# A fused attention, Fourier and gating kernel: batch 1's Fourier stage by radix 6 and 3, and GpSimd's products on VectorE

## The chip, the cores and the metric
One Trainium2 chip, one core of it. The metric is device microseconds of one launch. Engines in the text: PE (TensorE), DVE (VectorE), ACT (ScalarE), POOL (GpSimd), SP (which starts DMAs). Each engine runs its own list of instructions in order, so an instruction that waits holds back all behind it on that engine.

## What is computed
The reference runs three layers on 2 batches of 768 tokens. The first is a linear attention with decay over 8 heads of 48 features:

```
for t in range(S):
    cur = einsum('bhd,bhe->bhde', u * kt, vt)
    y[:, :, t] = einsum('bhd,bhde->bhe', rt, state + cur)
    state = wt[..., None] * state + einsum('bhd,bhe->bhde', kt, vt)
```

The second mixes by a Fourier transform over tokens and features, of which only the real part is kept, then normalises and runs an MLP (384 to 1536 to 384):

```
u  = x + real(fft(fft(x, axis=1), axis=2))
un = (u - mean(u)) / sqrt(var(u) + 1e-6)
x  = u + maximum(un @ w_ch1, 0) @ w_ch2
```

The third is a gated MLP: `h = gelu(x @ w_in)`, split in two halves, the second of them normalised and multiplied over the tokens by a 768x768 matrix `w_sg`, then `x + (u * v_s) @ w_out`. Inputs are 64-bit floats for the weights of the second and third layer.

## The kernel before, in words
**Precision.** Most of the large products are done as three passes over operands that are split in a high part (rounded, by ACT) and a low part (the difference): hi x hi, hi x lo, lo x hi. `divide` makes the two parts of the weights: a 64-bit weight arrives by DMA in `raw` (384 columns) or `w_raw` (768 columns), three DVE operations on its words (L170 to L172) make a 32-bit number in `st`, ACT copies it into `w.hi`, and POOL subtracts for `w.lo` (L177). There is one `st` tile, so the next weight's L170 can only begin when L177 has read it.

**Attention.** The heads go in pairs, four for each batch (n = 0 to 3 are batch 0, n = 4 to 7 batch 1). `prep` of a pair loads decays P (112x774), r and k (`rk`, or in one tile with P: XE, XO, prk) and v, and makes on DVE a scan of the decays (L232), a product with r (L245), and two products that make k (L249, L250); k times the inverse decays (L247) is on DVE for n = 0, 1 and on POOL for the others. `own_term` makes what a token takes from itself: for n >= 4 two products over `prod` on POOL (L264, L266), a sum on DVE (L267), and `times_v` on POOL (L279); for n < 4 by matmuls, a copy by ACT and `times_v` on POOL. `scores` are matmuls, an ACT copy and a mask by POOL (L294). `chunk_states` are transposes and matmuls, with a short scan on DVE (L319); `values` are matmuls and one addition on DVE (L344), half a pair at a time. `butterfly` adds and subtracts the halves of the tokens (L349, L350), with a high part by ACT and a low part by POOL (L352).

**Fourier stage.** `fourier` takes a batch through matrices of cosines and sines: 54 matmuls of 386 or 384 columns over the tokens (`x_ps`), 36 of 256 columns that put the own tokens in place (`t_ps`), and 72 of 192 or 194 columns over the features (`d_ps`).

**MLP of the second layer (`moe1`).** It goes over halves of a batch (384 tokens). A block is 9 matmuls of 384 columns into `z_ps`, a rounding by ACT (`z_hi`, L530), a difference by DVE (`z_lo`, L531), and 9 matmuls into `ch`. The third layer (`gating`) comes last.

**Order.** Written down, it is: batch 0's attention (span's start to about 75 us in the trace); batch 0's Fourier stage with the first steps of moe1 (75 to 101), whose instructions keep their written order, `first_through` being the last of them; then `merge(first(), second(), FR)`, which takes moe1's blocks of batch 0 in turn with the steps of batch 1: its attention (101 to 214) and its Fourier stage (214 to 262.6); then moe1 of batch 1, during which the weights `win` and `wsg` of the third layer are loaded and split, and the gating. Within this a scheduler with modelled times sets each engine's list, and it counts a tile's reuse and `behind(x, first_through)` as bounds. All of batch 1's preparation is held behind `first_through`; `attention` prepares one pair ahead (two at n = 0) and never beyond the running batch.

**Names the change touches:** KV and PV (which pairs have L247 and L264 on DVE), `divide` L177, `own_term` L266, `times_v` L279, `values` L344, `butterfly`, `attention`, `fourier` for batch 1, and the tables `tdft` (batch 0 and 1) in `load_tdft`.

Of the kernel before, what the change touches and what calls it, by code (L numbers as in the profile page):

```python
# [93 lines left out]
def fused(ctx, tc, ins, out, dbg=None):  # L94
# [104 lines left out]
    def prep(n, b, p, ap):  # L199
# [24 lines left out]
        for c0, c1 in parts:  # L224
# [98 lines left out]
    def values(b, c0, rt, sc, v, dv, U):  # L323
# [758 lines left out]
```

## Time and profile before

| what | value |
|---|---|
| median of 3 runs | 485.19 us (483.95 to 487.18) |
| the profiled execution's own time | 485.52 us |
| its span, first to last instruction | 483.7 us (1.8 us lie around it) |
| mean granted TensorE clock | 0.947 |
| busy: PE, DVE, POOL, ACT | 433.6, 274.0, 182.1, 172.7 us |
| chain that ended last: PE, DVE, issue, POOL, DMA, ACT | 55, 15, 10, 6, 5, 4% |

The profile is of one execution. Busy shares are means over stages with different limits, so the stretches are read apart: batch 0's attention, its Fourier stage, batch 1's attention with moe1 of batch 0, batch 1's Fourier stage, and what follows. A busy time of DVE or POOL includes time in which the other of the two held it up; a busy PE includes matmuls that wait in its pipe.

### The profile page before, as it was taken

The numbers are of one execution on the slowest core, as the hardware profiler recorded it, in microseconds if no ns is written. First come the engines' busy times: TensorE is split into PE (matmuls) and PEld (weight loads), VectorE is DVE, ScalarE is ACT, GpSimd is POOL, SyncE is SP. The second block draws the span as 40 slices with busy tenths as digits, with TensorE's granted clock in tenths as the row PEclk, the third lists the DMA queues.
The fourth block names the chain that finished last, engine by engine and source line by source line (L and its number), as shares of the span: only waits on it lengthen the run. The fifth ranks groups of instructions, "written<-read, shape, count | busy, mean of one in ns | idle before, by whom it ended". The sixth has DMA issues, their size and how long they took to land.

```text
span 483.7 us, 6884 instructions
## 1 busy us (share of the span) xinstructions
PE 433.6 (90%) x2662; PEld 408.3 (84%) x2662; DVE 274.0 (57%) x453; ACT 172.7 (36%) x369; POOL 182.1 (38%) x182
## 2 busy tenths in 40 slices
PE   8778788876789688999999799999998999999994
PEld 8667787765678678899999699999987998999994
DVE  4857387389986978634044963541158734711332
ACT  2435355452344236444322532431355413311110
POOL 2857553154786967320000341200446524200330
PEclk9659899897979989999999899999999999999998
DMA  8948534036035223013000041000243100110002
GB/s 213 251 146 265 166 119 130 0 101 242 0 119 176 91 67 110 1 40 91 1 0 2 1 131 33 1 0 1 66 114 88 61 1 1 43 56 1 0 20 87
DMA packets 14074, 36.75 MB, mean 76 GB/s; under 512 B 1808, under 2 KB 5680, under 8 KB 13648
## 3 DMA queue, kind: packets, MB, share of 16 engines
q1 hardware_dynamic: 13456, 32.54, 22.5%
q0 software_dynamic: 576, 3.68, 2.2%
q8 instruction: 23, 0.38, 0.3%
q14 instruction: 19, 0.16, 0.1%
HBM read 33.86 MB, written 2.36 MB: 75 GB/s over the span
## 4 chain that ended last, share of the span: by engine, by line
PE 55%; DVE 15%; issue 10%; POOL 6%; DMA 5%; ACT 4%; SPq 1%; POOLq 0%; ACTq 0%; DVEq 0%
PE s_ps L107 10%; PE ch L107 8%; PE z_ps L107 8%; PE o_ps L107 5%; PE u_ps L107 4%; PE d_ps L107 3%; PE x_ps L107 3%; PE v_ps L107 3%; PE t_ps L426 2%; PE y_ps L342 2%; DMA raw<-in_wsg 2%; DVE st L171 2%; DVE st L170 2%; DVE st L172 1%; DMA w_raw<-in_w 1%
## 5 line engine op out<-in xcount | busy, mean ns | idle before, releaser
L107 PE MATMUL ch<-z_hi,w 128*128 128x384 f32 x288 | 84.5, 355 | 3.9 <-DVE uT L541 2.3
L107 PE MATMUL z_ps<-us_hi,w 128*128 128x384 f32 x288 | 82.5, 348 | 0.8 <-ACT us_hi L506 0.5
L107 PEld LDWEIGHTS ch<-z_hi,w 128*128 128x128 f32 x288 | 55.4, 199 | 6.0 <-ACT z_hi L530 2.7
L107 PE MATMUL ch<-z_lo,w 128*128 128x384 f32 x144 | 51.3, 356 | 10.2 <-DVE z_lo L531 10.2
L531 DVE SCALAR_TENSOR_TENSOR z_lo<-z_ps,z_hi 128x384 fp32r<-128x384 f32 x48 | 26.4, 552 | 55.7 <-ACT z_hi L530 55.7
L107 PEld LDWEIGHTS z_ps<-us_hi,w 128*128 128x128 f32 x288 | 54.1, 193 | 2.2 <-ACT us_hi L506 0.8
L107 PE MATMUL z_ps<-us_lo,w 128*128 128x384 f32 x144 | 49.4, 343 | 0.0
L530 ACT ACTIVATE z_hi<-z_ps 128x384 fp32r<-128x384 f32 x48 | 23.4, 490 | 57.0 <-PE z_ps L107 43.8
L107 PEld LDWEIGHTS ch<-z_lo,w 128*128 128x128 f32 x144 | 28.5, 198 | 12.4 <-DVE z_lo L531 12.1
L623 POOL TENSOR_TENSOR vn_lo<-t_g,vn_hi 128x384 fp32r<-128x384 f32 x16 | 16.1, 1014 | 57.1 <-ACT vn_hi L622 57.1
L619 DVE SCALAR_TENSOR_TENSOR t_g<-s_ps,g,bsg 128x384 f32<-128x384 f32 x16 | 9.5, 615 | 43.6 <-PE s_ps L107 43.6
L294 POOL TENSOR_SCALAR_AFFINE_SELECT sc<-sc 128x384 f32<-128x384 f32 x32 | 29.5, 939 | 12.0 <-ACT sc L293 12.0
L342 PE MATMUL y_ps<-v,sc 128*128 128x120 f32 (+1 forms) x192 | 34.0, 301 | 0.0
L177 POOL TENSOR_TENSOR w<-st,w 128x384 fp32r<-128x384 f32 (+1 forms) x18 | 24.4, 1363 | 24.0 <-ACT w L176 23.9
L107 PE MATMUL s_ps<-wsg_hi,vn_lo 128*128 128x384 f32 x96 | 32.3, 336 | 0.0
L107 PE MATMUL s_ps<-wsg_hi,vn_hi 128*128 128x384 f32 x96 | 32.3, 336 | 0.0
L107 PE MATMUL s_ps<-wsg_lo,vn_hi 128*128 128x384 f32 x96 | 32.3, 336 | 0.0
L483 POOL TENSOR_TENSOR z_lo<-uc,z_hi 128x384 fp32r<-128x384 f32 x7 | 7.8, 1120 | 60.0 <-ACT z_hi L482 59.9
L342 PEld LDWEIGHTS y_ps<-v,sc 128*128 128x128 f32 x192 | 28.6, 209 | 1.2 <-issue 0.8
L107 PEld LDWEIGHTS z_ps<-us_lo,w 128*128 128x128 f32 x144 | 27.9, 194 | 0.0
L177 POOL TENSOR_TENSOR wsg_lo<-raw,wsg_hi 128x384 fp32r<-128x384 f32 x12 | 12.4, 1038 | 33.2 <-ACT wsg_hi L176 33.2
L622 ACT CAST vn_hi<-t_g 128x384 fp32r<-128x384 f32 x16 | 8.0, 513 | 38.9 <-DVE t_g L620 28.0
(261 smaller groups left out, 1060.0 us busy)
## 6 DMA issues: line engine op xcount, KB each, us to landing
raw<-in_w SPq DMA_DIRECT2D x12, 384.0 KB, 3.4
w_raw<-in_w SPq DMA_DIRECT2D x12, 384.0 KB, 4.5
raw<-in_win SPq DMA_DIRECT2D x8, 384.0 KB, 3.8
prod<-in_ruk SPq DMA_DIRECT2D x4, 624.0 KB, 4.6
tdft<-in_tdft POOLq DMA_DIRECT2D x2, 1158.0 KB, 6.8
v<-in_v SPq DMA_DIRECT2D x8, 288.0 KB, 5.7
raw<-in_wsg SPq DMA_DIRECT2D x12, 192.0 KB, 2.4
out<-o SPq DMA_DIRECT2D x12, 192.0 KB, 1.9
```

The costliest lines, as they stand in the source:

```text
L107: nc.tensor.matmul(o, lhsT=x, rhs=y, start=start and i == 0, stop=stop and i == len(ps) - 1, **kw)
L170: behind(nc.vector.tensor_scalar(out=st, in0=top, scalar1=3, scalar2=0x3FFFFFF8, op0=ALU.logical_shift_left, op1=ALU.bitwise_and), first_t ...
L171: nc.vector.scalar_tensor_tensor(out=st, in0=top, scalar=0xC0000000, in1=st, op0=ALU.bitwise_and, op1=ALU.bitwise_or)
L177: nc.gpsimd.tensor_tensor(out=w.lo[to], in0=x, in1=w.hi[to].bitcast(F32), op=ALU.subtract)
L294: nc.gpsimd.affine_select(out=sc, in_=sc, pattern=[[0, 3], [1, C]], compare_op=ALU.is_gt, fill=0.0, base=0, channel_multiplier=-1)
L342: nc.tensor.matmul(y3[:, i, to], lhsT=sc[h][:, i, :], rhs=vf[:, of], start=c == 0, stop=True, skip_group_check=c > 0)
L426: nc.tensor.matmul(o, lhsT=l, rhs=r, start=i == 0, stop=i == len(parts) - 1)
L530: nc.scalar.activation(out=z.hi, in_=z_ps, func=AF.Relu)
L531: nc.vector.scalar_tensor_tensor(out=z.lo, in0=z_ps, scalar=0.0, in1=z.hi.bitcast(F32), op0=ALU.max, op1=ALU.subtract)
L619: nc.vector.scalar_tensor_tensor(out=t, in0=s_ps[h], scalar=g[:, f:f + 1], in1=bsg[:, hs], op0=ALU.mult, op1=ALU.add)
L622: nc.scalar.copy(vn.hi[:, f, 3 * h:3 * h + 3], th)
L623: nc.gpsimd.tensor_tensor(out=vn.lo[:, f, 3 * h:3 * h + 3], in0=th, in1=vn.hi[:, f, 3 * h:3 * h + 3].bitcast(F32), op=ALU.subtract)
```

## The change
Five things change.

1. POOL's products move to DVE: L247 for all pairs (KV), L264 for all of batch 1 (PV), L266, `times_v` (which for n < 4 now reads the matmuls' result without ACT's copy), and the low parts of weights in `divide`.
2. The first two pairs of batch 1 (AP = 2) are prepared while batch 0's third and fourth pair run. Only later pairs' scans stay behind `first_through`; `dec` goes into the tile "kn", and there is a fourth `ends`.
3. Batch 1's `values` write straight into a tile of the whole batch, and `radix6` takes the place of `butterfly`: seven DVE additions a pair, none on ACT or POOL.
4. `fourier_by_radix` takes the place of `fourier` for batch 1: 18 transposes for the own tokens, `radix3` for three groups of frequencies (four DVE operations each), a split (high by ACT, low by DVE, 768 columns), 54 matmuls of 256 columns over the tokens, and 36 of 256 columns over the features, with the sums into `uT` on DVE.
5. Its table `dft6` (2.36 MB) is loaded once batch 0's Fourier stage has left the tile of `tdft`, by a DMA that POOL starts.

```diff
-KV = range(2)
+KV = range(8)
+AP = 2
-PV = range(1)
+PV = (0, *range(4, 8))
...
     def divide(w, to, x):
         nc.scalar.copy(w.hi[to], x)
-        nc.gpsimd.tensor_tensor(out=w.lo[to], in0=x, in1=w.hi[to].bitcast(F32), op=ALU.subtract)
+        nc.vector.tensor_tensor(out=w.lo[to], in0=x, in1=w.hi[to].bitcast(F32), op=ALU.subtract)
...
-            if b:
+            if n >= NP + AP:
                 behind(scan, first_through)
...
-            behind(own, first_through, mybir.DependencyClass.Sync)
-            nc.gpsimd.tensor_tensor(out=r, in0=r, in1=u.to_broadcast([C, NC_, 2 * D]), op=ALU.mult)
+            if n >= NP + AP - 1:
+                behind(own, first_through)
+            nc.vector.tensor_tensor(out=r, in0=r, in1=u.to_broadcast([C, NC_, 2 * D]), op=ALU.mult)
...
-        nc.scalar.copy(dg[:, :, :, 0], dg_ps[:, :2 * NC_].rearrange("p (c h) -> p c h", h=2))
-        times_v(dv, dg, v)
+        times_v(dv, dg_ps[:, :2 * NC_].rearrange("p (c h o) -> p c h o", h=2, o=1), v)
...
     def times_v(dv, dg, v):
-        nc.gpsimd.tensor_tensor(...)
+        nc.vector.tensor_tensor(...)
...
+        to = made(b)[0][:, c0:c0 + 3, es].rearrange("p i (h e) -> p i h e", h=2) if b else own
+        return nc.vector.tensor_tensor(out=to, in0=yh, in1=own, op=ALU.add)
...
+    def radix6(x, y, Z, es):
+        ya, yb = y[:, 0:3, es], y[:, 3:6, es]
+        nc.vector.tensor_tensor(out=x[:, 1, 0:3:2], in0=ya[:, 0:3:2], in1=yb[:, 0:3:2], op=ALU.subtract)
+        nc.vector.tensor_tensor(out=x[:, 1, 1], in0=yb[:, 1], in1=ya[:, 1], op=ALU.subtract)
+        nc.vector.tensor_tensor(out=x[:, 0, 0:3], in0=ya, in1=yb, op=ALU.add)
+        nc.vector.tensor_tensor(out=x[:, :, 3], in0=x[:, :, 1], in1=x[:, :, 2], op=ALU.add)
+        nc.vector.scalar_tensor_tensor(out=Z[:, 2:4, es], in0=x[:, :, 3], scalar=-0.5, in1=x[:, :, 0], op0=ALU.mult, op1=ALU.add)
+        nc.vector.tensor_tensor(out=Z[:, 4:6, es], in0=x[:, :, 1], in1=x[:, :, 2], op=ALU.subtract)
+        nc.vector.tensor_tensor(out=Z[:, 0:2, es], in0=x[:, :, 0], in1=x[:, :, 3], op=ALU.add)
...
-            for m in range(len(ready) + n, min(n + (3 if n == 0 else 2), (b + 1) * NP)):
+            for m in range(len(ready) + n, min(n + (3 if n in (0, NP - 2, NP - 1) else 2), len(pairs))):
...
+    def fourier_by_radix(b, ap, y, Z, uT, sdft, ddft):
+        yr = ap([C, NC_, C], "yr")
+        nc.scalar.copy(yr, y[:, :, DM - 1::-3])
+        for f in range(3):
+            for h in range(2):
+                t_ps = gps.tile([C, 512], F32, name="t_ps", tag="g")
+                for i in range(3):
+                    c = 3 * h + i
+                    nc.tensor.transpose(t_ps[:, i * C:(i + 1) * C], yr[:, c, :] if f == 2 else y[:, c, f::3], ident)
+                ...
+        yield
+        ...
+        def radix3(g):
+            W = Z[:, groups[g][0]].rearrange("p z (c j) -> p z c j", c=3)
+            s = ap([C, 2, C], "t")
+            nc.vector.tensor_tensor(out=s, in0=W[:, :, 1], in1=W[:, :, 2], op=ALU.add)
+            nc.vector.tensor_tensor(out=W[:, :, 2], in0=W[:, :, 1], in1=W[:, :, 2], op=ALU.subtract)
+            nc.vector.scalar_tensor_tensor(out=W[:, :, 1], in0=s, scalar=-0.5, in1=W[:, :, 0], op0=ALU.mult, op1=ALU.add)
+            nc.vector.tensor_tensor(out=W[:, :, 0], in0=W[:, :, 0], in1=s, op=ALU.add)
+            return W
+        def parts(n, W):
+            Ws = Split(ap([C, 2, 3, C], "Wh", F32R), ap([C, 2, 3, C], "W", F32R))
+            nc.scalar.copy(Ws.hi, W)
+            nc.vector.tensor_tensor(out=Ws.lo, in0=W, in1=Ws.hi.bitcast(F32), op=ALU.subtract)
+            return Ws
+        ...
+        for n, g in enumerate(order):          # order = (1, 2, 0)
+            ...
+            for w in range(3):
+                x_ps = gps.tile([C, 2, 2, C], F32, name="x_ps", tag="g")
+                ...                            # 6 mm3, of 256 columns, per w over the groups
+                nc.scalar.copy(X[w].hi[:, xo], x_ps[:, xi])
+                nc.vector.tensor_tensor(out=X[w].lo[:, xo], in0=x_ps[:, xi], in1=X[w].hi[:, xo].bitcast(F32), op=ALU.subtract)
+            prepare()
+            yield
+            ...
+            for f in range(2):                 # 2 mm3 for f = 0, 4 for f = 1, twice
+                ...
+                nc.scalar.copy(hs, gh[:, 1])
+                nc.vector.tensor_tensor(out=ds[:, 0], in0=gh[:, 0], in1=hs, op=ALU.subtract)
+                ...
+                nc.vector.tensor_tensor(out=to, in0=to, in1=ds[:, 0:k], op=ALU.add)
+                ...
+            yield
...
+        t = sh.tile([C, 2, 6, 3, C], F32R, name="dft6", tag="tdft")
+        nc.gpsimd.dma_start(out=t, in_=ins["dft6"].bitcast(F32R))
...
-            yield from fourier(1, f1_room, back, made(1), X1, uT[1], range(3))
+            yield from fourier_by_radix(1, f1_room, *made(1), uT[1], dft6[:, :, 0:2], dft6[:, :, 2])
```

The change also moves instructions within the lists, at three places that the prediction speaks of. The same code lies 2 or 3 lines further down in the changed kernel up to `chunk_states` (L170 is L172, L177 is L179, L245 is L247, L247 is L249, L266 is L269), 4 in `values` and `butterfly`, and 122 in moe1.

**DVE in the second half of batch 0's attention.** Before, from the first pair's butterfly on (XO holds r and k of n = 3, `raw` weights of moe1):

```order
L350 TENSOR_TENSOR kn<-dv 128x288
L344 TENSOR_TENSOR dv<-y_ps,dv 128x288
L249 SCALAR_TENSOR_TENSOR y_379,unit<-XO,y_379 112x768
L250 SCALAR_TENSOR_TENSOR XO<-y_379,XO 112x768
L319 SCALAR_TENSOR_TENSOR kn<-kn,dec 112x288
L344 TENSOR_TENSOR dv<-y_ps,dv 128x288
L349 TENSOR_TENSOR kn<-dv 128x288
L350 TENSOR_TENSOR kn<-dv 128x288
L344 TENSOR_TENSOR dv<-y_ps,dv 128x288
L170 TENSOR_SCALAR st<-raw 128x384
L171 SCALAR_TENSOR_TENSOR st<-raw,st 128x384
L170 TENSOR_SCALAR st<-raw 128x384
```

With the change, from the second pair's butterfly on (`prk` holds P, r and k of n = 5, `dg_ps` belongs to n = 3):

```order
L353 TENSOR_TENSOR kn<-dv 128x288
L354 TENSOR_TENSOR kn<-dv 128x288
L234 SCALAR_TENSOR_TENSOR prk<-prk,d_91 112x774
L281 TENSOR_TENSOR dv<-v,dg_ps 128x576
L247 SCALAR_TENSOR_TENSOR prk<-prk 112x768
L172 TENSOR_SCALAR st<-raw 128x384
L249 TENSOR_TENSOR prk<-prk,y_567 112x768
L173 SCALAR_TENSOR_TENSOR st<-raw,st 128x384
L172 TENSOR_SCALAR st<-raw 128x384
L251 SCALAR_TENSOR_TENSOR y_567,unit<-prk,y_567 112x768
L174 SCALAR_TENSOR_TENSOR st<-raw,st 128x384
L173 SCALAR_TENSOR_TENSOR st<-raw,st 128x384
```

The scan of the decays of n = 5 (L234) and the products that follow from it (L247, L249, L251) have come here, between batch 0's own work and its weights; before, all of batch 1's preparation stood behind `first_through`.

**DVE where moe1's blocks begin to run beside batch 1's attention.** Before (`w_raw` and `st` hold weights, `prod` r, k and u of a pair of batch 1, `var`, `rstd` and `uc` belong to moe1's normalisation):

```order
L245 SCALAR_TENSOR_TENSOR rk<-rk,P 112x768
L531 SCALAR_TENSOR_TENSOR z_lo<-z_ps,z_hi 128x384
L497 TENSOR_TENSOR uc<-uc,uT_84 128x384
L267 TENSOR_REDUCE dg<-prod 128x12
L170 TENSOR_SCALAR st<-w_raw 128x768
L249 SCALAR_TENSOR_TENSOR y_958,unit<-P,y_958 112x768
L171 SCALAR_TENSOR_TENSOR st<-w_raw,st 128x768
L250 SCALAR_TENSOR_TENSOR rk<-y_958,rk 112x768
L232 SCALAR_TENSOR_TENSOR prk<-prk,d_91 112x774
L172 SCALAR_TENSOR_TENSOR st<-w_raw,st 128x768
L520 SCALAR_TENSOR_TENSOR var<-var,rstd 128x384
L245 SCALAR_TENSOR_TENSOR prk<-prk 112x768
```

With the change:

```order
L269 TENSOR_TENSOR prod<-prod 128x576
L619 TENSOR_TENSOR uc<-uc,uT_84 128x384
L653 SCALAR_TENSOR_TENSOR z_lo<-z_ps,z_hi 128x384 x2
L270 TENSOR_REDUCE dg<-prod 128x12
L172 TENSOR_SCALAR st<-w_raw 128x768
L281 TENSOR_TENSOR dv<-v,dg 128x576
L173 SCALAR_TENSOR_TENSOR st<-w_raw,st 128x768
L174 SCALAR_TENSOR_TENSOR st<-w_raw,st 128x768
L179 TENSOR_TENSOR w_977<-st,w_977 128x768
L642 SCALAR_TENSOR_TENSOR var<-var,rstd 128x384
L172 TENSOR_SCALAR st<-w_raw 128x768
L643 SCALAR_TENSOR_TENSOR var<-var,rstd 128x384
```

The preparation (L245, L249, L250, L232) is gone from here; the products over `prod` and v (L269, L281) and the low parts of the weights (L179) have come from POOL.

**DVE at the start of batch 1's Fourier stage.** With the change (`AL` holds the six radix outputs Z, `prod` the low parts of a group):

```order
L517 TENSOR_TENSOR AL<-AL 128x2x128
L173 SCALAR_TENSOR_TENSOR st<-raw,st 128x384
L518 SCALAR_TENSOR_TENSOR AL<-sc,AL 128x2x128 x2
L173 SCALAR_TENSOR_TENSOR st<-raw,st 128x384
L653 SCALAR_TENSOR_TENSOR z_lo<-z_ps,z_hi 128x384
L644 SCALAR_TENSOR_TENSOR rstd<-var,rstd 128x384
L518 SCALAR_TENSOR_TENSOR AL<-sc,AL 128x2x128
L174 SCALAR_TENSOR_TENSOR st<-raw,st 128x384
L519 TENSOR_TENSOR AL<-AL,sc 128x2x128 x2
L174 SCALAR_TENSOR_TENSOR st<-raw,st 128x384
L519 TENSOR_TENSOR AL<-AL,sc 128x2x128
L525 TENSOR_TENSOR prod<-AL,P 128x768
```

Before, at this place stood the two butterfly additions of the last pair and then at once the low part of the first `x_ps`. Now `radix3` of three groups (L516 to L519) and five operations on weights (L172 to L174) stand ahead of the first low parts L525.

## Rows read from the trace of the kernel before

**Rows 1.** Busy time of each engine by stretch of the span.
```profile
core 0: us, PE busy (x) PEld busy (x) DVE busy (x) ACT busy (x) POOL busy (x), PEclk, DMA share, GB/s
0.00:75.00 75.00, 61.22 (x463) 54.79 (x463) 49.37 (x64) 30.64 (x68) 42.55 (x53) 0.84 0.68 196
...
101.00:214.00 113.00, 90.83 (x603) 80.87 (x601) 91.36 (x119) 46.07 (x96) 72.25 (x52) 0.92 0.29 97
214.00:262.60 48.60, 48.60 (x310) 48.60 (x310) 15.91 (x38) 14.74 (x36) 2.45 (x2) 1.00 0.12 33
262.60:320.00 57.40, 53.92 (x292) 52.04 (x291) 36.87 (x75) 23.06 (x50) 16.42 (x15) 0.97 0.12 35
```

**Rows 2.** Groups of DVE, 101 to 214 us; last column: idle before, releaser.
```profile
L170 DVE TENSOR_SCALAR st<-w_raw 128x768 uint32<-128x768 uint32 x6 | 6.5, 1078 | 2.3 <-POOL w L177 2.3
...
L344 DVE TENSOR_TENSOR dv<-y_ps,dv 128x288 f32<-128x288 f32 x7 | 3.1, 444 | 5.5 <-PE y_ps L342 5.5
...
L170 DVE TENSOR_SCALAR st<-raw 128x384 uint32<-128x384 uint32 x4 | 1.3, 352 | 3.3 <-POOL w L177 2.8 <-DMA raw<-in_w 0.5
```

**Rows 3.** Groups of POOL, 101 to 214 us, that the change leaves there.
```profile
L294 POOL TENSOR_SCALAR_AFFINE_SELECT sc<-sc 128x384 f32<-128x384 f32 x16 | 14.5, 918 | 4.0 <-ACT sc L293 4.0
...
L483 POOL TENSOR_TENSOR z_lo<-uc,z_hi 128x384 fp32r<-128x384 f32 x3 | 3.2, 1050 | 2.5 <-ACT z_hi L482 2.4
L511 POOL TENSOR_TENSOR uc<-uc 128x384 f32<-128x384 f32 x2 | 2.0, 1010 | 0.1
L510 POOL TENSOR_TENSOR uc<-uc 128x384 f32<-128x384 f32 x2 | 2.0, 1006 | 14.8 <-ACT uc L509 14.8
```

**Rows 4.** Timeline of DVE: start, us, operation, idle before.
```profile
117.53 1.75 DVE L232 TENSOR_TENSOR_SCAN prk<-prk,d 112x774 f32<-112x774 f32 x1
119.21 0.93 DVE L172 SCALAR_TENSOR_TENSOR st<-w_raw,st 128x768 uint32<-128x768 uint32 x1
120.06 0.55 DVE L520 SCALAR_TENSOR_TENSOR var<-var,rstd 128x384 f32<-128x384 f32 x1
120.53 0.94 DVE L245 SCALAR_TENSOR_TENSOR prk<-prk 112x768 f32<-112x768 f32 x1
...
123.20 3.73 DVE L170 TENSOR_SCALAR st<-w_raw 128x768 uint32<-128x768 uint32 x1 [0.66 <-POOL w L177]
```

**Rows 5.** Timeline of POOL beside the last row of the group before.
```profile
123.12 1.54 POOL L247 TENSOR_TENSOR prk<-prk,y 112x768 f32<-112x768 f32 x1
...
125.11 1.40 POOL L264 TENSOR_TENSOR prod<-prod 128x576 f32<-128x576 f32 x1
```

**Rows 6.** Chain that ended last: start, us, engine and line.
```profile
44.84 1.15 POOL dv L279
45.99 1.50 POOL XO L247
...
55.78 5.96 DMA raw<-in_w
...
223.35 1.60 PE x_ps L107 x9
224.96 2.04 PE t_ps L426 x12
226.99 1.56 PE z_ps L107 x9
...
236.75 1.99 PE d_ps L107 x18
```

**Rows 7.** Timeline of DVE, end of batch 1's attention.
```profile
214.23 0.46 DVE L344 TENSOR_TENSOR dv<-y_ps,dv 128x288 f32<-128x288 f32 x1 [1.27 <-PE y_ps L342]
...
218.85 0.36 DVE L170 TENSOR_SCALAR st<-raw 128x384 uint32<-128x384 uint32 x1 [2.29 <-DMA raw<-in_win]
```

**Rows 8.** DMA issues: KB each, median us from issue to landing.
```profile
rk<-in_rk SPq DMA_DIRECT2D x2, 672.0 KB, 4.8
...
XO<-in_rk SPq DMA_DIRECT2D x1, 672.0 KB, 14.3
```

More of the change, by code (lines that the diff above doesn't have):

```diff
@@ L250, in prep @@
             ready_k.append(nc.vector.scalar_tensor_tensor(out=k, in0=flat(y0), scalar=2.0, in1=k, op0=ALU.subtract, op1=ALU.mult))
-        ends = all_ends[n % 3]
+        ends = all_ends[n % 4]
         nc.scalar.copy(ends[:, 0:NC_ - 1], P[:, 0:NC_ - 1, C])
@@ L313, in chunk_states @@
                 nc.tensor.matmul(kv_ps[r0:r1, c * D:c * D + C], lhsT=kn[:, c, r0:r1], rhs=vf[:, o:o + C], start=True, stop=True)
-        us = ap([PR, D, NC_], "kn")
+        both = ap([PR, 2, D, NC_], "kn")
+        us, dec = both[:, 0], both[:, 1]
+        nc.scalar.copy(dec, ends[:, None, :].to_broadcast([PR, D, NC_]))
         nc.scalar.copy(us, kv_ps[:, :NC_ * D].rearrange("p (c e) -> p e c", c=NC_))
-        nc.scalar.copy(dec[:, :, 0:NC_ - 1], ends[:, None, 0:NC_ - 1].to_broadcast([PR, D, NC_ - 1]))
         chain = us.rearrange("p e c -> p (e c)")
@@ L369, in tail @@
                 region = len(nc.cur_bb.bb.instructions)
-            gate = values(b, 3, rt, sc[2:], v, dv, states[n % 2])
-            butterfly(ap, dv, made(b), slice(p * 2 * D, (p + 1) * 2 * D), nc.vector if b == 0 and p == NP - 1 else nc.gpsimd)
+            gate = values(b, 3, rt, sc[2:], v, dv, states[n % 2], slice(p * 2 * D, (p + 1) * 2 * D))
+            es = slice(p * 2 * D, (p + 1) * 2 * D)
+            if b:
+                radix6(ap([C, 2, 4, 2 * D], "kn"), *made(b), es)
+            else:
+                butterfly(ap, dv, made(b), es, nc.vector if p == NP - 1 else nc.gpsimd)
             through(b, p)
@@ L392, in attention @@
             yield
-            values(b, 0, rt, sc[:2], v, dv, states[n % 2])
+            values(b, 0, rt, sc[:2], v, dv, states[n % 2], slice(p * 2 * D, (p + 1) * 2 * D))
             last = (n, b, p, rt, sc, v, dv)
@@ L850, in fused @@
         states = [sh.tile([PR, NC_ - 1, 2 * D], F32, name=f"U{i}") for i in range(2)]
-        all_ends = [sh.tile([PR, NC_], F32, name=f"ends{i}") for i in range(3)]
-        dec = sh.tile([PR, D, NC_], F32, name="dec")
-        for t in (*states, *all_ends, dec):
+        all_ends = [sh.tile([PR, NC_], F32, name=f"ends{i}") for i in range(4)]
+        for t in (*states, *all_ends):
             nc.gpsimd.memset(t, 0.0)
@@ L862, in fused @@
         a_room = room(att.enter_context(tc.tile_pool(name="att", bufs=1)), CFG1)
-        f1_room = room_of(a_room, ps="v", su="dv")
+        f1_room = room_of(a_room, yr="y0", Wh="P", W="prod", Xh="rk", t="sc", ds="dv")
         parts, X0 = {}, [[], []]
@@ L867, in made @@
             if b not in parts:
-                parts[b] = parts_of(f_room if b == 0 else a_room)
+                parts[b] = parts_of(f_room) if b == 0 else [a_room([C, NC_, DM], t) for t in ("AH", "AL")]
             return parts[b]
@@ L1003, in _constants @@
         fd[:, 2 * i], fd[:, 2 * i + 1] = np.cos(ph), -np.sin(ph)
+    k3 = -math.sqrt(3.0) / 2
+    cols = []
+    for r, z in ((0, "r"), (3, "r"), (1, "r"), (1, "i"), (2, "r"), (2, "i")):
+        th = 2 * np.pi * ((p[:, None] * (6 * p[None, :] + r)) % S) / S
+        c, s = np.cos(th), np.sin(th)
+        g = k3 if r == 2 else -k3
+        cols.append(np.concatenate([c, s], 1) if z == "r" else g * np.concatenate([s, -c], 1))
+    sd = np.stack(cols, 1)
+    ph0 = 2 * np.pi * ((p[:, None] * (3 * p[None, :])) % DM) / DM
+    ph1 = 2 * np.pi * ((p[:, None] * (3 * p[None, :] + 1)) % DM) / DM
+    dd = np.stack([np.cos(ph0), np.sin(ph0), np.cos(ph1), k3 * np.sin(ph1), -k3 * np.cos(ph1), np.sin(ph1)], 1)
     half = np.zeros((C, 2, 2, 2, C // 2), np.float32)
```

68 lines of the change are left out of this document (58 added, 10 removed).

## The prediction, made before the changed kernel had run

> **What bounds the kernel now.** I read first the busy table by stretch [rows 1], to see which engine is full where. Four stretches matter. In batch 0's attention (0 to 75 us) no engine is full: PE 61.2, DVE 49.4 and POOL 42.6 of 75. In batch 1's attention beside moe1 (101 to 214, 113 us) DVE is busy 91.4, PE 90.8, POOL 72.3. In batch 1's Fourier stage (214 to 262.6) PE is busy all of 48.6. After that PE has 53.9 of 57.4, DVE 36.9.
>
> Second, the groups of DVE in the second stretch [rows 2]: part of its 21.6 us of idle time ends on POOL (2.3 and 2.8, both times the first step of the next weight, which waits until POOL has read `st`), 5.5 on PE's result of the values. Third, DVE's timeline [rows 4]. Where nothing disturbs it, a 774-wide scan takes 1.68 us from its start to the next start, a 768-wide operation 0.85, a 384-wide one 0.47; I use 0.07 + columns/960 us for other widths. But the one-input L170 of 768 columns, at 123.20, took 3.73, over four times the price of the two-input operation of that width, and beside it POOL ran L247 and L264 [rows 5]. So DVE's busy time contains waiting that POOL causes. Priced at the quiet rates, the 116 operations that DVE runs in that stretch would take 65.4 us, not 91.4: 26 us are stretch. Fourth, the chain [rows 6] for what orders batch 0's attention and the Fourier stage.
>
> **The change, part by part.**
>
> *A, batch 0's attention and Fourier stage (0 to 101).* By the new order DVE runs 84 operations up to the end of the attention instead of 58; the added ones (preparation of n = 4 and 5, k of n = 2 and 3, four `times_v`, low parts of weights) cost 20 us at quiet prices, against 25.6 of idle. The chain loses POOL's `times_v` and k, 1.15 and 1.50 [rows 6], for 0.67 and 0.85 on DVE: about 1.2 here, and as much again where the same pair of steps recurs. But near 55 us the chain passes to a DMA of weights (5.96), and n = 5's preparation now stands in front of those weights' DVE work, which gives most of it back. I take −1. Bounds: −2.7 (POOL's steps vanish, nothing comes back), and +16, if of the 20 us only the 4 of removed stretch are covered; I am near the low end because idle time exceeds the addition and DVE is the only engine that gets work.
>
> *B, batch 1's attention beside moe1 (113 us).* DVE's list from the first block to the last addition of the values, at quiet prices:
> - was 65.4
> - preparation of n = 4 and 5, now in A: −8.9; butterflies −2.6; small operations of the normalisation and sums that fall on the other side of the cut −2.6
> - three radix6 of seven operations +5.6; k for n = 6 and 7 +1.7; products over `prod` +4.0; `times_v` +2.0; ten low parts of weights +7.1
>
> The sum is 71.7, say 72. To it comes what stretch is left. POOL keeps its masks and the LayerNorm pieces, 14.5 + 3.2 + 2.0 + 2.0 = 21.7 us [rows 3] of 72.3; taking stretch in proportion, 26 x 21.7/72.3 = 7.8. Of the idle 21.6, the 5.1 behind POOL go [rows 2]; 16.5 stay, since PE's results come no sooner. That makes 72 + 7.8 + 16.5 = 96, or −17. Bounds: no idle at all gives 80, −33; PE's own work speaks against that (90.8 busy, though that contains waiting). On the other side, all of POOL's 21.7 stops DVE: 72 + 21.7 + 16.5 = 110, −3. I take −17, the proportional case: what POOL keeps are short operations (0.9 to 1.05 us [rows 3]) spread over the stretch, where the removed ones ran in pairs, 1.54 and 1.40 one behind the other [rows 5].
>
> *C, batch 1's Fourier stage (48.6 us).* PE spends 6 x 1.60 on `x_ps`, 3 x 2.04 on `t_ps` and 4 x 1.99 on `d_ps`: 23.7 us [rows 6]; moe1's blocks take the rest and stay. The change makes 90 matmuls of 256 columns. From 1.60/9 = 0.178 for 386 columns, a 256-wide one is 0.12 (bounds: 0.111, the 192-wide ones of `d_ps`, and 0.170, the 256-wide ones of `t_ps`): 10.8, and 18 transposes in 6 groups at 0.16: 2.9. PE saves 10. But the operands now come by DVE: from the last value to the first low part (L525) stand 24 or so operations, namely radix6 (1.9), radix3 of three groups (4.0), a weight pair (2.4), rows of the normalisation (1.4) and two of 0.55 and 0.86, about 12 us, and that weight pair has to wait for its DMA: in the kernel before DVE idled 2.3 us for it at 218.85, all 4.6 us from the last values to it in hand [rows 7]. PE has 2.9 us of transposes and 3.2 of one block (18 matmuls at 1.56/9 [rows 6]) to cover it. I count 5.5 of waiting and 2 more where a group's gh, hs and sums run one after the other with one block to hide them. −10 + 7.5 = −2.5, say −3. Bounds −9.5 (0.5 exposed) and +4.3 (the whole 12 and a DMA of 2.3 exposed).
>
> *D, after 262.6.* 24 low parts of 384 columns go to DVE at 0.47, 11 us of work, on an engine busy for 36.9 of 57.4 [rows 1]; PE, with 53.9 of 57.4, sets the end. 0; if that idle cover of 20 us were gone, part of the 11 would show: bounds −2 and +4. The table's DMA of 2.36 MB starts after batch 0's Fourier stage, in a stretch whose DMA share is 0.29 [rows 1], more than 100 us ahead of its use: 0.
>
> Sum: −1 − 17 − 3 + 0 = −21, so a span of 462.7; with the 1.8 around it 464.5. The profiled execution is 0.3 us above the median of 485.19, so the median of the new kernel comes to **464**.
>
> **A rule of the chip against it.** The row at 123.20 shows DVE slowed by POOL, with an operation that has a single input. The Trainium skill, page "SBUF — State Buffer", section "Who interferes with whom", says that DVE and GpSimd share a port pair as an exclusive lock: the second fully blocks for the whole instruction, and DVE operations with two SBUF inputs contend with every GpSimd instruction that reads SBUF. By that rule the products that move are all of the contending kind, and what POOL keeps would stop them in full, which is the first rival; that L170, with one input, was held too agrees with what the section says of `tensor_scalar` in its two-port modes.
>
> **Rivals.**
> 1. *POOL's remainder blocks DVE whole.* For it: the 3.73 us; against it: most of DVE's quiet-priced operations ran undisturbed though POOL was busy 64% of the stretch. B gives −3 in place of −17: 478. Chance 0.12.
> 2. *The Fourier chain is exposed.* Radix work, weights and their DMA wait stand in one line on DVE, C becomes +4.3: 471.3. For it: DVE waits in order, and the row at 218.85; against it: the transposes and a block of moe1 need nothing of that line. Chance 0.08.
> 3. *DVE's idle goes too.* Without POOL in the loop of weights and values, PE's next block starts sooner and 16.5 us of idle shrink to 3: 450.5. Against it: PE is then at its own 90.8 of work. Chance 0.12.
> 4. *Slower: DVE's list stands still in batch 0's attention.* Three loads that DVE's in-order list needs (r and k, P, and `prod` of batch 1's first pairs) are now queued on SP and waited for on DVE in front of batch 0's work and its weights. Such a load takes 4.8 us, or 14.3 where many are in flight (XO) [rows 8], and in this stretch the DMA share is 0.68 [rows 1]. Were DVE held for 9.5 (the difference) at each of three loads, A costs +28.5 instead of −1: 464 + 29.5 = 493.5. It decides against the change from about 21 us of waiting on. Against it: scan and products of n = 4 stand behind batch 0's own values, and 25.6 us are idle. Chance 0.05.
> 5. *No change:* DVE's added work is as long as the stretch it saves, 485. Chance 0.03.
>
> **How the numbers follow.** The forecast case has 0.60; its own range is 456 to 472, from the bounds of C and half those of B. The range that should hold 8 in 10 reaches down into rival 3 and up to rival 1: 452 to 479. A measurement can tell about 1%, 4.85 us. Faster by that: the forecast, rivals 1 to 3 without the edge of rival 1, 0.88; the same: that edge and rival 5, 0.07; slower: rival 4, 0.05.
>
> **What would show it.** A: the end of batch 0's Fourier stage stays near 100 us, and DVE up to there is busier by some 16. B: 768-wide operations at 0.85 without cases like 3.73; POOL's busy time over the span falls from 182 to under 100; the last values of batch 1 lie 18 us sooner. C: PE has one visible gap of 4 to 8 us ahead of the first `x_ps`, and the stage lasts about 46. D: the stretch from there to the end keeps its 221 us. I am wrong if DVE waits for DMAs before 75 us, if masks stretch DVE as the products did, or if PE's gap in C exceeds 12 us.

## The result, and the profile after

The changed kernel takes 468.56 us (median of 4 runs, 466.4 to 469.11) against 485.05; ratio 0.9647, 95% interval 0.9602 to 0.9691. The forecast was 464, range 452 to 479: right in direction and range, 4.6 us too low. The profiled execution took 468.74 us with a span of 467.0, so 16.7 us of span are to be accounted for. Of the four executions of run 10 below, two ran throughout at a granted clock of 0.65 (583 and 584 us), and its times leave them out.

The two traces are cut at the same four events: the first `x_ps` matmul behind batch 0's last values (A0 ends), the first `us_lo` of moe1 (batch 0's Fourier stage, AF, ends), batch 1's last values (B ends), and the last addition into batch 1's `uT` (C ends); the rest is D. The busy time of each engine in these stretches, before:

```profile
core 0: us, PE busy (x) PEld busy (x) DVE busy (x) ACT busy (x) POOL busy (x), PEclk, DMA share, GB/s
0.00:71.24 71.24, 57.81 (x445) 51.70 (x446) 45.75 (x58) 29.58 (x65) 40.05 (x51) 0.83 0.68 197
71.24:99.81 28.57, 25.37 (x152) 23.35 (x152) 16.47 (x36) 13.19 (x34) 6.49 (x6) 0.94 0.21 56
99.81:214.23 114.42, 92.25 (x614) 82.29 (x614) 92.55 (x122) 47.26 (x98) 72.25 (x52) 0.93 0.29 96
214.23:264.68 50.45, 50.36 (x318) 50.04 (x316) 17.99 (x44) 15.44 (x38) 2.45 (x2) 1.00 0.11 32
264.68:483.70 219.02, 207.76 (x1139) 200.89 (x1139) 101.29 (x197) 67.25 (x136) 60.82 (x71) 0.98 0.13 39
```

and after:

```profile
core 0: us, PE busy (x) PEld busy (x) DVE busy (x) ACT busy (x) POOL busy (x), PEclk, DMA share, GB/s
0.00:76.20 76.20, 60.35 (x445) 55.02 (x446) 63.69 (x86) 33.81 (x69) 33.06 (x43) 0.82 0.72 207
76.20:104.69 28.49, 26.27 (x152) 24.66 (x152) 15.27 (x37) 12.24 (x32) 0.58 (x1) 0.88 0.23 66
104.69:199.17 94.48, 84.94 (x603) 77.00 (x602) 78.72 (x143) 40.95 (x86) 17.91 (x23) 0.95 0.35 119
199.17:237.36 38.19, 33.42 (x195) 31.44 (x194) 26.27 (x59) 14.42 (x30) 0.00 (x0) 0.87 0.14 42
237.36:467.00 229.64, 220.25 (x1221) 213.22 (x1220) 112.35 (x230) 70.69 (x142) 37.49 (x48) 1.00 0.12 37
```

These lengths mislead on their own, because moe1's blocks have moved between the stretches. A half block is nine matmuls, six of them with `us_hi` or `z_hi`; so the matmul groups count them. In stretch C, before:

```profile
L107 PE MATMUL z_ps<-us_hi,w 128*128 128x384 f32 x54 | 15.3, 337 | 0.0
L107 PE MATMUL ch<-z_hi,w 128*128 128x384 f32 x51 | 14.3, 337 | 0.0
```

and after:

```profile
L109 PE MATMUL z_ps<-us_hi,w 128*128 128x384 f32 x33 | 10.3, 373 | 0.0
L109 PE MATMUL ch<-z_hi,w 128*128 128x384 f32 x24 | 6.9, 341 | 0.6 <-ACT z_hi L652 0.6
```

That is (54 + 51)/6 = 17.5 half blocks before and 9.5 after. At 1.56 us a half block [rows 6] the table takes them out ("at equal work" is the length less 1.56 times the half blocks in it):

| stretch | half blocks before, after | at equal work before | after | change | forecast |
|---|---|---|---|---|---|
| A0, attention of batch 0 | 0, 0 | 71.2 | 76.2 | +5.0 | −1 with AF |
| AF, its Fourier stage | 0, 0 | 28.6 | 28.5 | −0.1 | |
| B, attention of batch 1 | 29, 28 | 69.2 | 50.8 | −18.4 | −17 |
| C, its Fourier stage | 17.5, 9.5 | 23.2 | 23.4 | +0.2 | −3 |
| D, the rest | 49.5, 58.5 | 141.8 | 138.4 | −3.4 | 0 |

The sum is −16.7. B went as forecast, 1.4 beyond it; A lost 6 us more, C gained 3 less, D gained 3.4 more.

In B, what answers to [rows 2] and [rows 3]: the groups of DVE

```profile
L179 DVE TENSOR_TENSOR w<-st,w 128x768 fp32r<-128x768 f32 (+1 forms) x10 | 7.9, 790 | 2.7 <-ACT w L178 2.7
...
L172 DVE TENSOR_SCALAR st<-w_raw 128x768 uint32<-128x768 uint32 x6 | 3.5, 582 | 0.0
L172 DVE TENSOR_SCALAR st<-raw 128x384 uint32<-128x384 uint32 x4 | 1.3, 350 | 0.0
```

and of POOL

```profile
L296 POOL TENSOR_SCALAR_AFFINE_SELECT sc<-sc 128x384 f32<-128x384 f32 x16 | 10.9, 703 | 48.8 <-ACT sc L295 48.8
L605 POOL TENSOR_TENSOR z_lo<-uc,z_hi 128x384 fp32r<-128x384 f32 x3 | 3.1, 1018 | 17.1 <-ACT z_hi L604 17.1
```

The first weight step of 768 columns takes 582 ns instead of 1078 and waits for nobody, where it waited 2.3 us for POOL. The masks, unchanged, take 703 ns instead of 918. DVE busy is 78.7 (forecast 72 + 7.8) and its idle time 15.8 (forecast 16.5).

The stretch can be taken from the traces directly. I take as quiet the lower quartile of the durations of each operation and shape in B over the kernels of this study, and add up what each instruction took beyond it; this sum is called stretch below. It is 25.0 us before, 5.3 after.

In C, the granted clock in small windows after the last values (199.17):

```profile
203.00:207.00 4.00, 2.61 (x14) 1.97 (x12) 4.00 (x12) 1.55 (x4) 0.00 (x0) 1.00 0.08 31
207.00:210.00 3.00, 1.45 (x7) 1.13 (x7) 3.00 (x8) 0.83 (x1) 0.00 (x0) 0.87 0.19 20
210.00:213.00 3.00, 3.00 (x14) 3.00 (x15) 1.15 (x3) 0.37 (x1) 0.00 (x0) 0.50 0.71 246
213.00:216.00 3.00, 2.29 (x11) 2.00 (x10) 1.89 (x4) 1.48 (x3) 0.00 (x0) 0.50 0.01 2
216.00:219.00 3.00, 3.00 (x12) 3.00 (x11) 0.06 (x1) 0.00 (x0) 0.00 (x0) 0.50 0.00 0
219.00:222.00 3.00, 3.00 (x21) 3.00 (x21) 1.67 (x4) 2.32 (x5) 0.00 (x0) 0.93 0.00 0
```

From 203 to 210 DVE is busy without a pause, PE for 4.1 of these 7 us; then, when the operands are there, TensorE runs at half clock (1.2 of 2.4 GHz) for some 10 us. PE's first token matmuls, 10.7 us after the last values:

```profile
209.87 1.65 PE L109 MATMUL x_ps<-dft,P 128*128 128x256 f32 x6 [1.14 <-ACT P L524]
```

### The profile page after: what moved, and what is told of

Read it like the earlier page. It is cut to its first block, busy times and chain, and to the rows that moved or that the text cites. A ratio compares the mean times of both kernels' runs of the same rounds, so it can differ in the third digit from the quotient of the medians.

```text
span 467.0 us, 6782 instructions
## 1 busy us (share of the span) xinstructions
PE 425.2 (91%) x2608; PEld 401.3 (86%) x2608; DVE 296.3 (63%) x552; ACT 172.1 (37%) x358; POOL 89.0 (19%) x115
## 3 DMA queue, kind: packets, MB, share of 16 engines
HBM read 36.22 MB, written 2.36 MB: 83 GB/s over the span
## 4 chain that ended last, share of the span: by engine, by line
PE 69%; DVE 15%; DMA 5%; ACT 3%; issue 2%; DVEq 0%; ACTq 0%
PE ch L109 14%; PE z_ps L109 12%; PE s_ps L109 11%; PE u_ps L109 5%; PE o_ps L109 5%; PE v_ps L109 5%; PE x_ps L109 3%; PE y_ps L345 3%; PE sc_ps L292 2%; DVE st L173 2%; PE kv_ps L315 2%; PE d_ps L109 2%; PE y_ps L336 2%; DMA raw<-in_win 2%; PE t_ps L446 2%
## 5 line engine op out<-in xcount | busy, mean ns | idle before, releaser
L109 PE MATMUL ch<-z_hi,w 128*128 128x384 f32 x288 | 81.3, 343 | 6.3 <-ACT z_hi L652 3.4
L109 PE MATMUL z_ps<-us_hi,w 128*128 128x384 f32 x288 | 81.4, 346 | 0.0
L109 PEld LDWEIGHTS ch<-z_hi,w 128*128 128x128 f32 x288 | 53.1, 191 | 8.4 <-ACT z_hi L652 4.3
L109 PE MATMUL ch<-z_lo,w 128*128 128x384 f32 x144 | 50.1, 348 | 5.9 <-DVE z_lo L653 5.8
L652 ACT ACTIVATE z_hi<-z_ps 128x384 fp32r<-128x384 f32 x48 | 23.4, 490 | 67.0 <-PE z_ps L109 56.2
L296 POOL TENSOR_SCALAR_AFFINE_SELECT sc<-sc 128x384 f32<-128x384 f32 x32 | 28.1, 898 | 65.9 <-ACT sc L295 65.9
L109 PEld LDWEIGHTS ch<-z_lo,w 128*128 128x128 f32 x144 | 27.5, 191 | 8.3 <-DVE z_lo L653 8.2
L109 PEld LDWEIGHTS s_ps<-wsg_lo,vn_hi 128*128 128x128 f32 x96 | 18.0, 188 | 0.1
L109 PEld LDWEIGHTS s_ps<-wsg_hi,vn_hi 128*128 128x128 f32 x96 | 18.0, 188 | 0.1
```

The lines of the kernel that those rows point to most:

```text
L109: nc.tensor.matmul(o, lhsT=x, rhs=y, start=start and i == 0, stop=stop and i == len(ps) - 1, **kw)
L296: nc.gpsimd.affine_select(out=sc, in_=sc, pattern=[[0, 3], [1, C]], compare_op=ALU.is_gt, fill=0.0, base=0, channel_multiplier=-1)
L652: nc.scalar.activation(out=z.hi, in_=z_ps, func=AF.Relu)
```

## The experiments

All are edits of the changed kernel; the cuts show the lines that matter, and `...` stands for what is left out. Ratios are to the kernel before, run on the same chip. The changed kernel's is 0.9647.

**1. Without the early preparation.**

```diff
-AP = 2
+AP = 0
-  ... min(n + (3 if n in (0, NP - 2, NP - 1) else 2), len(pairs))
+  ... min(n + (3 if n == 0 else 2), (b + 1) * NP)
```

> The changed kernel (468.6 us) without the early preparation of batch 1's first two pairs (AP = 0). Theory (DVE's work decides both stretches): batch 0's part gets its 4.9 us back, the stretch of batch 1's attention gets the 8.9 us of preparation on DVE, so about 472 to 473. Rival (the gain of that stretch comes from the early start of batch 1's attention, not from less stretch on DVE): most of the 18 us gained there are lost again, 480 or more. Second rival (the early preparation costs more than it brings): 464 or less.

Measured 469.27, ratio 0.9706 (0.963 to 0.9782). Its two attention stretches:

```profile
0.00:66.80 66.80, 57.30 (x446) 52.11 (x446) 46.22 (x64) 29.20 (x61) 29.00 (x43) 0.87 0.71 210
94.65:206.61 111.96, 95.69 (x612) 84.65 (x611) 92.94 (x162) 46.58 (x95) 21.96 (x23) 0.88 0.33 109
```

A0 is 9.4 us shorter than with the early preparation, B at equal work 15.9 longer (DVE 92.9 instead of 78.7), C 3.9 shorter. Against the kernel before, B gains only 2.5 us here, though stretch is down to 4.1 us: DVE exchanged 21 us of waiting for 25 us of work (at the quiet durations). So the early preparation is what made room in B, and it took most of that from A0; in whole times it is not to be told from nothing. My number missed by 3, and both rivals fell.

**2. The low parts of weights back on POOL.**

```diff
-        nc.vector.tensor_tensor(out=w.lo[to], ...)
+        nc.gpsimd.tensor_tensor(out=w.lo[to], ...)
```

> The changed kernel with the low parts of all weights back on POOL. Theory: in batch 1's attention DVE loses 7.1 us of work but gets some 6 us of stretch beside POOL and 5 us of waiting for POOL at the next weight, +4 there, and +3 after the Fourier stages, where the next weight again waits for POOL: about 475. Rival (DVE is simply full, whatever POOL does): DVE has 7 us less to do, 462. Rival (no effect, PE decides): 468.6.

Measured 473.53, ratio 0.9825 (0.9754 to 0.9897). Against the changed kernel B at equal work is +2.2 (expected +4) and D +3.5 (expected +3). In B DVE waits 5.5 us for POOL at the next weight, as expected, but stretch is only 7.9 us, 2.6 more and not 6. In D the trace shows no such wait; PE's idle time there is 1.3 longer, and the granted clock is 0.99 instead of 1.00. C, whose DVE list ahead of the first token matmuls is the changed kernel's, is 3.4 shorter, at a granted clock of 1.00:

```profile
200.88:235.72 34.84, 29.84 (x195) 27.75 (x195) 26.17 (x59) 14.36 (x30) 0.00 (x0) 1.00 0.15 46
211.60 0.97 PE L109 MATMUL x_ps<-dft,P 128*128 128x256 f32 x6 [1.14 <-ACT P L524]
```

The first token matmuls come 10.7 us after the last values, as in the changed kernel, with the same wait ahead of them.

**3. The products back on POOL.** KV, PV, L269 and `times_v` as before.

```diff
-KV = range(8)
-PV = (0, *range(4, 8))
+KV = range(2)
+PV = range(1)
...
-            nc.vector.tensor_tensor(out=r, in0=r, in1=u.to_broadcast([C, NC_, 2 * D]), op=ALU.mult)
+            nc.gpsimd.tensor_tensor(out=r, in0=r, in1=u.to_broadcast([C, NC_, 2 * D]), op=ALU.mult)
```

> The changed kernel with the products of k, of the own term and with v back on POOL as before (weights' low parts stay on DVE). Theory: DVE loses about 8 us of work in batch 1's attention and gets as much stretch, and the chain gets POOL's slower products: 470 to 476. Rival (stretch is no matter, DVE's own work counts): 460. Rival (what POOL does on the chain is the whole gain): 478 or more.

Measured 478.41, ratio 0.9878 (0.981 to 0.9946): the products are the larger half of the moves. In B stretch rises from 5.3 to 15.2 us while DVE has 12 operations fewer; B at equal work +7.6. It came out 2 us above the theory's range, at the edge of the rival's; that POOL's slower products on the path count beside the stretch is likely but not shown.

**4. Batch 1's Fourier stage as before.** `fourier(1, ...)` and the butterflies in place of the radix functions.

> The changed kernel with batch 1's Fourier stage and butterflies as before (matmuls of 386 and 194 columns). Theory from the two traces, at equal work of the second layer: the new stage gains about nothing (10 us less of matmuls against 5 us of PE waiting and 4 to 5 us at half clock), and the radix additions cost DVE 3 us in batch 1's attention: 466 to 470. Rival (the new stage is worth its 10 us): 478.

Measured 469.22, ratio 0.9731 (0.9664 to 0.9798): by the medians the radix stage, as the change has it, is worth 0.7 us, by the ratios 4, and their intervals overlap; it is not to be told from nothing, though it saves 8 to 9 us of PE's work (23.1 us beside the blocks in C before, 15.0 in run 2 and 14.3 in run 7, both at a clock of 1.00).

**5 and 6. POOL work that nobody waits for.** Four operations of 576 columns behind the masks, eight times in batch 1's attention, on a table no longer in use.

```diff
+    def extra(b):
+        for i in range(4 if b else 0):
+            x = nc.gpsimd.tensor_tensor(out=idle[i % 2], in0=idle[0], in1=idle[1], op=ALU.mult)   # run 5
+            x = nc.gpsimd.memset(idle[i % 2], 0.0)                                                # run 6
+            behind(x, mask)
```

> The changed kernel with 32 more POOL products of 128x576 (two inputs in SBUF) during batch 1's attention, in fours behind the masks; nobody reads their results, and they write over a table that is no longer used. They are some 45 us of POOL work, and no instruction of another engine waits for them. Theory (POOL's running work stretches DVE): before, 72 us of POOL work stood beside 26 us of stretch, so DVE gets up to 16 us longer in this stretch and the kernel 10 to 16 us, 479 to 485; 768-wide DVE operations of 2 us and more appear. Rival (POOL only matters where something waits for its result): 468 to 471.

> The same 32 places, but POOL fills the same 576 columns with zeros, which reads nothing from SBUF. If the stretch comes from the reading, DVE's operations keep their quiet durations and the kernel takes 468 to 471. If any POOL work stretches DVE, it grows by a third of POOL's added time, 5 to 10 us. The Trainium skill, page "SBUF — State Buffer", section "Who interferes with whom", says that a DVE instruction with two SBUF inputs contends with a GpSimd instruction that reads SBUF and not with one that only writes it; by that sentence this run shows no stretch.

Measured 497.3 (ratio 1.0252, 1.0167 to 1.0337) with the products, 467.18 (0.9631, 0.9542 to 0.972) with the fills. DVE's and POOL's groups in B, with the products:

```profile
L173 DVE TENSOR_SCALAR st<-w_raw 128x768 uint32<-128x768 uint32 x6 | 5.2, 868 | 0.1
L250 DVE TENSOR_TENSOR rk<-rk,y 112x768 f32<-112x768 f32 x1 | 2.2, 2183 | 0.0
L307 POOL TENSOR_TENSOR fdft<-fdft 128x576 fp32r<-128x576 f32 x32 | 58.1, 1816 | 1.8
```

and with the fills:

```profile
L173 DVE TENSOR_SCALAR st<-w_raw 128x768 uint32<-128x768 uint32 x6 | 3.4, 573 | 0.0
L250 DVE TENSOR_TENSOR rk<-rk,y 112x768 f32<-112x768 f32 x1 | 0.9, 950 | 0.0
L307 POOL MEMSET fdft<- 128x576 f32 x32 | 17.1, 576 | 0.0
```

and stretch B as a whole, with the products and with the fills:

```profile
100.40:226.36 125.96, 96.82 (x603) 86.95 (x602) 102.07 (x143) 40.60 (x86) 82.56 (x55) 0.82 0.26 89
```
```profile
102.96:196.80 93.84, 86.79 (x603) 77.97 (x602) 78.92 (x142) 40.90 (x86) 38.95 (x55) 0.93 0.34 120
```

The same 142 or 143 DVE instructions take 102.1 us in the one and 78.9 in the other; stretch is 28.1 and 5.4 us. The product L250 takes 2183 ns beside reading POOL work and 950 beside writing. This settles it: POOL's running slows DVE without any dependency, and it is the products, which read, that do it and not the fills, which only write. The fills are shorter in all (17.1 us against 58.1), but at a third of that they would have cost 6 us, and L250 lay wholly beside fills. Here the Trainium skill's sentence (page "SBUF — State Buffer", section "Who interferes with whom") agrees with the runs. B grew by 31.5 us, 8.7 more than the stretch. Two things beside it can have cost that, and I did not separate them: moe1's `z_lo` queues behind the products on POOL (PE's matmuls into `mu` wait 6.2 us for it), and TensorE's granted clock in B is 0.82 instead of 0.95. The forecast of 10 to 16 us was too small.

Over the kernels, stretch goes with POOL's busy time in B, where that reads: 25.0 of 72.3 us before, 16.6 of 58.7 (run 9), 15.2 of 40.3 (run 3), 28.1 of 82.6 (run 5), 5.3 of 17.9 (changed kernel), 7.9 of 38.1 (run 2), 4.1 of 22.0 (run 1): between 0.19 and 0.38 us for each us of POOL, so no fixed price.

**7. Only what the first group needs stands ahead of it.**

```diff
+            x = nc.vector.tensor_tensor(out=s, in0=W[:, :, 1], in1=W[:, :, 2], op=ALU.add)
+            behind(x, low[-1] if low else None)
...
+            nonlocal first_through
+            first_through = nc.vector.tensor_tensor(out=Ws.lo, ...)     # later weights wait for it
+            low.append(first_through)
```

> The changed kernel with one change of order at batch 1's Fourier stage: the radix-3 operations of the second and third group wait for the low part of the group before, and the weights of the third layer wait for the last group's low part. So between the last values and the first low part stand 5.1 us less of DVE work. Theory: PE's first token matmul comes 4 to 5 us sooner, PE's gap is shorter, and part of the 4 us at half clock go too: 460 to 465. Rival (the chain is set by ACT's rounding or the DMA of the table, not by DVE's list): 468. Rival (the weights come late and the stage after loses it again): 468, with the Fourier stage shorter and the rest longer.

Measured 462.53, ratio 0.9527 (0.947 to 0.9583): faster than both kernels, by 6 us against the changed one. Stretch C:

```profile
198.82:230.26 31.44, 28.89 (x194) 27.53 (x193) 26.92 (x63) 14.38 (x30) 0.00 (x0) 1.00 0.16 51
```

with PE's first token matmuls

```profile
206.82 0.87 PE L109 MATMUL x_ps<-dft,P 128*128 128x256 f32 x6
```

They begin 8.0 us after the last values instead of 10.7, and six of them take 0.87 us where they took 1.65 at half clock. C at equal work is 16.9 instead of 23.4: PE's idle time in C is 2.2 less (2.6 instead of 4.8), and the other 4.3 are PE's own time, at a clock of 1.00 instead of 0.87. The first token matmuls come 2.7 us sooner, not 4 to 5. Against run 2, whose clock in C is 1.00 too, C gains 3.1.

**8. The fifth pair's preparation moved into batch 0's Fourier stage.**

```diff
+            elif n == NP + 1:
+                behind(scan, gate)        # the last values of batch 0
...
-  ... min(n + (3 if n in (0, NP - 2, NP - 1) else 2), len(pairs))
+  ... min(n + (3 if n in (0, NP - 2) else 2), len(pairs))
```

> The changed kernel, but the fifth batch-1 step of preparation order is altered: the scan of pair n = 5 waits for the last values of batch 0, so its DVE work falls into batch 0's Fourier stage, where DVE is busy 15 of 28 us. Theory (DVE's list in the second half of batch 0's attention sets its end): that attention ends 4 to 5 us sooner, the Fourier stage grows by 0 to 2, batch 1's attention stays: 464 to 466. Rival (the attention of batch 0 is set by the DMAs of the weights and by PE at the lower clock): 468 to 470.

Measured 474.28, ratio 0.975 (0.9679 to 0.982): slower by 5. A0 is 2.7 us shorter, but AF 4.0 and B 5.6 longer. Idle time of DVE in AF was no cover; that the written order there is one chain, into which the added work went, is my reading and not shown. Both my theory and the rival were wrong.

**9. Early preparation and radix stage, with all of POOL's old work back on POOL.** The edits of runs 2 and 3 together.

> The changed kernel with the early preparation and the radix stage, but with all of POOL's old work back on POOL (products, times_v, low parts). It closes a square with the kernel without early preparation (469.3) and the changed kernel (468.6), where the products' return alone cost 9 and the low parts' return alone 5. Theory (the early preparation pays only if DVE is free of POOL's stretch): 480 to 485, as long as the kernel before, with 20 us or more of stretch on DVE in batch 1's attention. Rival (the early preparation alone carries the gain): 470 to 474.

Measured 485.34, ratio 1.0024 (0.9981 to 1.0067): the kernel before. The two attention stretches:

```profile
0.00:79.70 79.70, 58.11 (x445) 52.88 (x446) 59.48 (x68) 33.35 (x71) 51.46 (x56) 0.83 0.63 188
108.53:214.25 105.72, 89.02 (x603) 80.18 (x602) 75.89 (x121) 40.43 (x86) 58.68 (x44) 0.90 0.31 107
```

B at equal work gains 7.1 and A0 loses 8.5. So the early preparation and the radix stage bring nothing without the moves. Stretch in B is 16.6, not the 20 expected.

**10. Batch 1's masks as a DVE product from PSUM,** on top of run 7.

```diff
+            if b:
+                nc.vector.tensor_tensor(out=sc, in0=sc_ps, in1=below[:, None, :].to_broadcast([C, 3, C]), op=ALU.mult)
+                res.append(sc)
+                continue
```

> The kernel with the altered order at the radix stage (462.5), and batch 1's masks as one DVE product from the scores' PSUM with a 0/1 tile, in place of an ACT copy and a POOL mask: 16 DVE operations of 384 columns at 0.5 us, 8 us more DVE work against POOL's last 13 us of masks. Theory (what stretch is left comes from the masks, and their way through ACT and POOL is on PE's path): DVE's stretch of 6 us goes, two steps become one, 456 to 461. Rival (DVE is the bound of that stretch whatever POOL does): 465 to 470.

Measured 463.35 and 466.88, too few for an interval. DVE's stretch in B falls to 2.4 us, but its busy time rises from 78.5 in run 7 to 83.1 and B at equal work from 50.7 to 53.5. No gain; whether there is a loss stays open.

**11 and 12. One early pair, and none, on top of run 7.**

```diff
-AP = 2
+AP = 1        # run 11, with the second pair left to batch 1's loop
+AP = 0        # run 12, with the edit of run 1
```

> The kernel with the altered order at the radix stage (462.5), but only the first pair of batch 1 prepared early (AP = 1); the second waits for batch 0's Fourier stage as before. Theory (DVE is full from 40 us to the end of batch 0's attention and again in batch 1's): about 4.5 us of DVE work move from the one to the other, batch 0's attention ends 3 to 4 us sooner, batch 1's grows by 5 to 8: 464 to 467. Rival (the second pair's preparation is the one in the way): 459 to 461.

> No early preparation (AP = 0, 469.3) together with the altered order at the radix stage (the changed kernel with that order alone: 462.5; with one early pair: 462.6). Theory (the early preparation only shifts DVE's work from one full stretch to another, and is worth nothing): 462 to 465, the Fourier stage some 3 to 5 us shorter than without the order. Rival (early preparation is worth several us once the Fourier stage is mended): 467 or more.

Measured 462.58 (0.9523, 0.9464 to 0.9582) and 465.01 (0.9556, 0.9486 to 0.9626), against 0.9527 with two. A0 shrinks with each pair taken out (76.3, 71.9, 67.9 us) and B at equal work grows (50.7, 60.4, 66.8). The second pair is worth nothing, the first not more than can be measured. In run 12 stretch C at equal work is 13.1 against 19.5 in run 1.

## Why the prediction was right, and where its terms were off

**The mechanism of B held, in size too.** The step that carried the forecast was that DVE's busy time before contained 26 us of waiting caused by POOL, that the moves replace it by DVE work of about the same size, and that the preparation taken out shortens the list. The traces give 25.0 us of stretch before and 5.3 after (forecast 7.8), idle 15.8 (16.5), and B −18.4 (−17); batch 1's last values come 15.1 us sooner, not 18, since A is later. Runs 5 and 6 show that it is contention and not waiting for results; run 9 that without the moves nothing is left of the gain; run 1 that without the early preparation the moves still give 14 us, but in other stretches: against the kernel before A0 −4.4, AF −0.7, B −2.5, C −3.7, D −3.2.

**The total has luck in it.** D's gain was not forecast, and it hides part of the losses in A and C: without it the time would have been some 8 us above the forecast, not 4.6.

**The rivals.** A full block by POOL's remainder was wrong: its 17.9 us left in B cost DVE 5.3. The exposed Fourier chain was half right (a gap of 4.8 us, and the clock). That DVE's idle goes too was wrong, 15.8 us stayed. No change at all is what run 9 shows for the change without its moves; POOL's busy time over the span fell from 182 to 89 us, as the prediction asked.

**A was mis-sized: −1 forecast, +4.9 measured.** The step that failed is "idle time exceeds the addition". I compared 20 us of new work with 25.6 us of idle in all of A0. But the new pairs' work can only fall behind the earlier pairs', and there DVE has now become full. A0 from 40 us on, before and after:

```profile
40.00:71.24 31.24, 25.28 (x223) 22.63 (x222) 19.57 (x31) 15.93 (x34) 18.67 (x20) 0.95 0.61 188
40.00:76.20 36.20, 26.86 (x213) 24.86 (x210) 34.41 (x52) 18.37 (x38) 15.38 (x12) 0.86 0.63 191
```

DVE's busy time there grew by 14.8 us. The idle time in reach was 11.7, of which 1.8 are left, so 9.9 are covered and 5.0 are not. The size has an uncertainty: runs 5 and 6 have the same DVE list up to here as the changed kernel and end A0 at 72.0 and 74.0, so the 5.0 of one profile is 1 to 5. The cause is shown by runs 1, 11 and 12: A0 is 66.8 and 67.9 without early pairs, 71.9 with one, 76.2 and 76.3 with two. TensorE's granted clock does not explain it: run 10, with two and a clock of 0.89 in A0, has 75.6, the kernel before 71.2 at 0.83.

**C: −3 forecast, +0.2 measured.** The matmuls saved 8 to 9 us, not 10, and the waiting of PE was 38.2 − 33.4 = 4.8, less than my 7.5. What I did not have is the clock: PE worked about 10 us at half speed, some 4 us lost. Its size varies from execution to execution: with the same gap runs 5 and 6 show 21.1 and 20.8 at equal work at a clock of 0.95, and run 2 shows 20.0 at 1.00, which is −3.2, the forecast. So at full clock the sum came out, with two terms each some 2 us too large that cancel, and what missed is the clock of this execution. Run 7 confirms that DVE's list ahead of the first low part sets the gap: with less in front of it 2.2 of its 4.8 us are gone. What decides between half and full clock after a gap of this length is open.

**D: 0 forecast, −3.4 measured.** I had counted the low parts on DVE as added work only. By the rows of D, 1.9 of the 3.4 are idle time of PE (11.3 before, 9.4 after); the other 1.5 are PE's own time, at a granted clock of 0.98 before and 1.00 after, and no gain of the change that is shown. Over the runs D is 141.8 to 142.4 where the low parts are on POOL (before, runs 2 and 9) and 138.0 to 140.9 in all others, so the sign is shown and the size is not. The wait that I expected to see go, DVE's for POOL at the next weight, is 2.9 us in D before and 0 after, but 0 in run 2 as well.

**Slower:** the DMA waits in batch 0's attention that would have made it slower did not come (DVE waits 6.3 us for DMAs in A0, 7.1 before); the loss in A is DVE's own fullness.

## What to carry to other kernels

A busy VectorE beside a busy GpSimd is not a measure of work: price the instructions at their quiet durations, and the difference is what moving GpSimd's reading operations away can give, less what they cost on VectorE. Look for idle time where the moved work can stand, not over the stage. And when a stage saves matmuls but gets its operands through another engine's list, put in front of the first operand only what it needs: the wait can be paid twice, once as a gap (4.8 us here) and once in the clock after it (some 4 us in one execution, nothing in another).

## What was not expected of the hardware

GpSimd's fill of 128x576 took 576 ns and stretched VectorE by nothing that shows (5.4 us against 5.3), while the products of the same width, 1816 ns each, cost VectorE 22.8 us for 64.7 us more of GpSimd's busy time, about a third; even a VectorE operation with one input, the weight step of 128x768, went from 573 to 868 ns in the mean (none of the six lay beside a fill in run 6, so for one input the fill is untested). TensorE, after 4.1 busy us of 7, was granted half its clock from about 209 to 219 us; in run 7, with a shorter gap at the same place, it kept 1.00, and in run 2, with the same gap, it kept 1.00 too.
